# Softmax-off-by-one attention and a maxout feed-forward on one core: the first batch's attention in two query halves, in a hand-made order

## The chip, the cores and the metric

The kernel runs on one NeuronCore of a Trainium2 chip. The metric is the device time of one execution in microseconds (us). Each comparison states the ratio of two kernels: the mean time of one kernel's fast runs over the mean of the other's of the same rounds, with a 95% interval; it is therefore not exactly the ratio of the medians that are quoted beside it. The three batches of experiments were made on different chips, so kernels of two batches are best compared by what each gained on the kernel before in its own batch. The "granted clock" is the share of TensorE's full clock that the throttle let through in an execution. Engines: PE (TensorE, matmuls), ACT (ScalarE), DVE (VectorE), POOL (GpSimd, which here only starts loads), SP (SyncE, starts stores and DMA transposes).

## The reference

Batch 8, 12 heads, 448 tokens, head size 64; then a feed-forward over all 8 x 448 = 3584 tokens of width 768. All inputs and the output are fp32.

```python
scores = scale * np.matmul(q, k.transpose(0, 1, 3, 2))
m = np.max(scores, axis=-1, keepdims=True)
e = np.exp(scores - m)
attn = e / (np.sum(e, axis=-1, keepdims=True) + np.exp(-m) + 1e-09)   # = exp(s) / (1 + sum exp(s))
x = (attn @ v).transpose(0, 2, 1, 3).reshape(B * S, H * D)
h = np.maximum(np.maximum(x @ w1, x @ w2), x @ w3)
out = h @ w_out
```

## The kernel before

The 12 heads of a batch are three groups of four, so there are 24 groups. For each group the kernel makes four "score visits"; each visit issues two key chunks' scores for a pair of heads (PE) and two exponentials (ACT). The denominator and numerator ("AV") of group i-1 are issued in the second visit of group i. Feed-forward "pieces" of the previous batch (18 up-projection pieces, then 6 or 8 output pieces) are put between the visits by a credit of matmul columns, so that PE has work while ACT makes exponentials. A piece of batch b can only be issued when the attention of batch b is complete. So in batch 0 there are no pieces at all.

```python
    ps1 = ctx.enter_context(tc.tile_pool(name="ps1", bufs=4, space=bass.MemoryType.PSUM))  # transposes, AV, pieces
    ps2 = ctx.enter_context(tc.tile_pool(name="ps2", bufs=2, space=bass.MemoryType.PSUM))  # scores, 2 banks each
    ...
    def pair_qk(i):                 # copies of q and k into the order that the transposes want, on DVE
        ...
        for pr in range(GH // 2):
            qk16 = p16_pool.tile([SC, 2, NCH, 2, D], MMDT, tag="qk16", name="qk16")
            for n, t in enumerate((kf, qf)):
                nc.vector.tensor_copy(out=qk16[:, n], in_=t[:, 2 * pr : 2 * pr + 2].rearrange("p h c d -> p c h d"))
    ...
    def av_group(i):
        ...
        den = col_tiled(lambda hh, c: ones16[:, :])
        nc.scalar.activation(out=lnd, in_=den[:, 0:S], func=AF.Ln, bias=one_b)
        nc.scalar.activation(out=rb, in_=lnd, func=AF.Exp, bias=ln_lam, scale=-1.0)
        for hf in range(2):
            num = col_tiled(lambda hh, c: v16[:, hh, c, hf::2])
            nc.vector.tensor_tensor(out=xT[b][:, 2 * g + hf, :], in0=num[:, 0:S], in1=rb, op=ALU.mult)
    ...
    for i in range(NI):
        ...
        gap = (per_group + av_cols + 2 * tr) / 4
        for vi, (pr, cs) in enumerate(visits):
            if vi == 1 and i > 0:
                av_group(i - 1)
            scores_visit(i, pr, cs)
            if vi == 0:
                if on_pe:
                    pair_qk(i + 1)          # all four copies of the next group, ahead of xT's products on DVE
                ...
                moe(gap - av_cols)
            elif vi < 3:
                if vi == 1 and i > 0 and g == 0:
                    add_pieces(b - 1)
                moe((gap - tr) / 2)
                if on_pe:
                    pe_transpose_pair(i + 1, vi - 1)
                moe((gap - tr) / 2)
            else:
                moe(gap)
```

The softmax here doesn't subtract the row's maximum and nothing guards it: scores larger than these inputs give would overflow.

## Time and profile before

The kernel takes 367.57 us (median of 3 runs, 367.45 to 367.81). The profile is of one execution in the slow state (more than 1.5% above the fastest, at a lower granted clock): 407.0 us at a granted TensorE clock of 0.852. Its table of windows gives, for each stretch of the span, the busy time of each engine (with the number of instructions), then the granted clock, the DMA share and GB/s:

```profile
10.00:20.00 10.00, 8.13 (x60) 3.17 (x63) 3.07 (x10) 8.27 (x11) 4.24 (x7) 1.00 1.28 190
30.00:40.00 10.00, 8.02 (x90) 3.37 (x85) 2.50 (x4) 8.02 (x11) 4.16 (x7) 0.74 1.22 205
40.00:50.00 10.00, 10.00 (x70) 4.36 (x62) 5.53 (x12) 3.45 (x4) 4.54 (x7) 0.79 1.28 203
100.00:150.00 50.00, 50.00 (x366) 21.17 (x368) 23.01 (x50) 26.25 (x33) 6.25 (x9) 0.85 0.66 101
350.00:390.00 40.00, 40.00 (x265) 18.46 (x263) 17.50 (x30) 9.51 (x12) 0.00 (x0) 0.85 0.10 31
```

From about 42 us on, PE (first of the busy times) is without a break; ACT (fourth) is about half busy, and less near the end. Before that PE and ACT both show 8 of 10 us. The chain of waits names what sits in that head (start, length, what):

```profile
13.74 3.46 ACT eT L176 x4
17.80 4.13 PE av L196 x47
22.27 4.96 ACT eT L176 x6
27.64 4.08 PE av L196 x48
32.05 4.96 ACT eT L176 x6
37.43 3.91 PE av L196 x48
42.00 2.73 PE p_i L226 x12
56.60 2.74 PE av L196 x48
```

The exponentials (ACT) and the AV blocks (PE) take turns. An AV block takes about 4 us here and 2.74 us later, because PE is at half clock: 93 ns for one of its matmuls is 112 columns (a quarter of 448, as four 32-column tiles run together) at 1.2 GHz. The Trainium skill ("TensorE: Matmul & The Clock Gate", Part 1) says that PE drops to this clock when it has had too little work. The clock column shows 1.00 in the first of these windows although PE is at half clock there: the clock record of this trace begins only with the first change to the higher clock, at 21.1 us.

### The profile page before, as it was taken

How to read it: one execution, taken by the hardware profiler on the slowest of the kernel's cores; microseconds unless marked ns; L12 is line 12 of the kernel's file. 1: busy time of each engine (PE TensorE's matmuls, PEld its weight loads, DVE VectorE, ACT ScalarE, POOL GpSimd, SP SyncE). 2: the span in 40 equal slices, each digit the busy share in tenths (PEclk: the TensorE clock that was granted, in tenths of full speed). 3: DMA queues.
4: the chain of work that ended last, by engine and by line, in shares of the span. 5: the costliest groups of instructions: out<-in, count | busy, mean ns of one | idle time of the engine just before them, and what ended most of it. 6: DMA issues, size and time to landing. Idle time of an engine off the chain costs nothing.

```text
span 407.0 us, 6789 instructions
## 1 busy us (share of the span) xinstructions
PE 389.1 (96%) x2832; PEld 167.4 (41%) x2832; DVE 176.1 (43%) x359; ACT 196.4 (48%) x241; POOL 59.4 (15%) x92
## 2 busy tenths in 40 slices
PE   2888999999999999999999999999999999999995
PEld 1333444443434434344344444444344444344442
DVE  2332554444444444444443444444444443434442
ACT  2887353663644645554545454644645635541000
POOL 8444420220201202201202202202000000000000
PEclk9977888888888888888888888888888888888888
DMA  7999996756838935566437848278212510012005
GB/s 90 192 206 205 202 173 102 110 146 89 112 40 155 156 82 69 89 163 93 75 61 135 150 86 105 54 148 143 48 22 52 156 41 0 2 56 62 0 2 155
DMA packets 73470, 40.94 MB, mean 101 GB/s; under 512 B 35680, under 2 KB 68704, under 8 KB 73440
## 3 DMA queue, kind: packets, MB, share of 16 engines
q0 software_dynamic: 35552, 21.24, 38.0%
q1 hardware_dynamic: 37888, 19.28, 20.7%
q8 instruction: 22, 0.36, 0.4%
q14 instruction: 8, 0.07, 0.1%
HBM read 42.47 MB, written 11.01 MB: 131 GB/s over the span
## 4 chain that ended last, share of the span: by engine, by line
PE 92%; ACT 3%; DMA 2%; POOL 1%; issue 0%; DVE 0%; POOLq 0%
PE p_i L226 48%; PE av L196 17%; PE op_ps L247 16%; PE stp L167 11%; ACT eT L176 3%; DMA ld_k<-in_k_dram 2%; PE trT L141 1%; POOL ld_q L88 1%; POOL ld_k L88 0%; DVE o_sb L254 0%; DVE qk_170 L129 0%; POOL ident_97 masks.py:199 0%; POOL ident_97 masks.py:197 0%; POOLq L366 0%
## 5 line engine op out<-in xcount | busy, mean ns | idle before, releaser
L176 ACT ACTIVATE eT<-stp 112x896 f16<-112x896 f32 x192 | 164.7, 916 | 156.0 <-PE stp L167 156.0
L236 DVE TENSOR_TENSOR hT<-hT,p_i 128x448 f16<-128x448 f16 x96 | 59.6, 621 | 80.6 <-PE p_i L226 80.6
L226 PE MATMUL p_i<-xT,w_122 128*128 128x448 f16 x288 | 70.8, 387 | 0.0
L226 PE MATMUL p_i<-xT,w_123 128*128 128x448 f16 x288 | 70.7, 388 | 0.0
L226 PE MATMUL p_i<-xT,w_124 128*128 128x448 f16 x288 | 70.2, 387 | 0.0
L247 PE MATMUL op_ps<-w_125,hT 128*128 128x384 f16 x336 | 66.5, 358 | 0.0
L167 PE MATMUL stp<-qkT 64*128 64x448 f16 x384 | 59.9, 385 | 5.5 <-ACT eT L176 5.4
L196 PE MATMUL av<-eT,ld_v 112*32 112x448 f16 x768 | 49.5, 408 | 0.0
L254 DVE TENSOR_SCALAR o_sb<-op_ps 128x384 f32<-128x384 f32 x56 | 31.2, 558 | 39.8 <-PE op_ps L247 39.8
L88 POOL DMA_DIRECT2D ld_v<-in_v_dram x24 | 16.8, 702 | 213.1 <-PE stp L167 136.2
L212 DVE TENSOR_TENSOR xT<-av,rb 128x448 f16<-128x448 f32 x48 | 27.9, 620 | 45.1 <-ACT rb L209 37.4
L234 DVE CAST hT<-p_i 128x448 f16<-128x448 f32 x48 | 30.0, 625 | 39.7 <-PE p_i L226 39.7
L247 PEld LDWEIGHTS <-hT 128*128 128x128 f16 x336 | 33.7, 104 | 32.4 <-issue 7.1
L226 PEld LDWEIGHTS <-w_123 128*128 128x128 f16 x288 | 28.6, 104 | 35.3 <-issue 7.3
L226 PEld LDWEIGHTS <-w_124 128*128 128x128 f16 x288 | 27.7, 103 | 36.4 <-issue 9.3
L226 PEld LDWEIGHTS <-w_122 128*128 128x128 f16 x288 | 27.9, 103 | 35.5 <-issue 7.9
L196 PEld LDWEIGHTS <-ld_v 112*32 112x32 f16 x768 | 22.5, 108 | 22.7 <-issue 4.3
L167 PEld LDWEIGHTS <-qkT 64*128 64x128 f16 x384 | 12.1, 95 | 46.7 <-issue 46.1
L196 PE MATMUL av<-eT,ones_116 112*32 112x448 f16 x384 | 25.6, 393 | 0.0
L207 ACT ACTIVATE lnd<-av,one_b 128x448 f32<-128x448 f32 x24 | 15.3, 638 | 14.9 <-PE av L196 14.8
L88 POOL DMA_DIRECT2D ld_q<-in_q_dram x25 | 17.7, 708 | 6.8 <-DMA w_124<-in_moe_w_dram 1.5
L88 POOL DMA_DIRECT2D ld_k<-in_k_dram x25 | 17.5, 698 | 5.2 <-DMA ld_v<-in_v_dram 1.9
(137 smaller groups left out, 84.7 us busy)
## 6 DMA issues: line engine op xcount, KB each, us to landing
ld_v<-in_v_dram POOLq DMA_DIRECT2D x24, 224.0 KB, 4.5
ld_q<-in_q_dram POOLq DMA_DIRECT2D x23, 224.0 KB, 5.6
ld_k<-in_k_dram POOLq DMA_DIRECT2D x23, 224.0 KB, 6.2
out_dram<-o_sb SPq DMA_DIRECT2D x8, 336.0 KB, 2.8
out_dram<-o_sb SPq DMA_DIRECT2D x8, 288.0 KB, 2.6
out_dram<-o_sb SPq DMA_DIRECT2D x8, 240.0 KB, 2.7
out_dram<-o_sb SPq DMA_DIRECT2D x8, 192.0 KB, 2.6
w_122<-in_moe_w_dram POOLq DMA_DIRECT2D x3, 384.0 KB, 10.6
```

What stands on the lines that cost most here:

```text
L88: nc.gpsimd.dma_start(out=tiles[name][:, h0 : h0 + step].rearrange("p h c d -> p h (c d)"), in_=src[:, h0 : h0 + step],)
L141: nc.tensor.transpose(out=trT[:, n, ts(c, SC)], in_=qk16[:, n, c, :, :], identity=ident16[0:SC, 0:SC],)
L167: nc.tensor.matmul(out=stp[:, hh, 0:S], lhsT=qkT[hh * D : hh * D + D, c * SC : c * SC + 128], rhs=qkT[hh * D : hh * D + D, S : 2 * S], sta ...
L176: nc.scalar.activation(out=st["eT"][:, 2 * pr : 2 * pr + 2, c, :], in_=stp[0:SC, :, 0:S], func=AF.Exp, scale=scale,)
L196: nc.tensor.matmul(out=bank[32 * hh : 32 * hh + 32, 0:S], lhsT=weights(hh, c), rhs=eT[:, hh, c, :], start=(c == 0), stop=(c == NCH - 1),)
L207: nc.scalar.activation(out=lnd, in_=den[:, 0:S], func=AF.Ln, bias=one_b)
L212: nc.vector.tensor_tensor(out=xT[b][:, 2 * g + hf, :], in0=num[:, 0:S], in1=rb, op=ALU.mult)
L226: nc.tensor.matmul(out=p_i[:, 0:S], lhsT=w_sb[i][:, dc, ts(fc, 128)], rhs=xT[b][:, dc, :], start=(dc == 0), stop=(dc == NDC - 1),)
L234: nc.vector.tensor_copy(out=dst, in_=p_i[:, 0:S])
L236: nc.vector.tensor_tensor(out=dst, in0=dst, in1=p_i[:, 0:S], op=ALU.max)
L247: nc.tensor.matmul(out=op_ps[:, 0:NW], lhsT=hT[bp][:, fc, ts(t, 128)], rhs=wout_sb[:, fc, ts(nh, NW)], start=(fc == 0), stop=(fc == NFC - 1),)
L254: nc.vector.tensor_scalar(out=o_sb[:, ts(nh, NW)], in0=op_ps[:, 0:NW], scalar1=1.0 / LAMBDA, scalar2=None, op0=ALU.mult,)
```

## The change

The intent is to have feed-forward work for PE earlier. Batch 0's attention is computed for the first 224 queries of all three groups first. Then up-projection pieces for those 224 tokens are legal, and the hand-made order puts seven of them under the second half's exponentials. Besides: the first two heads' q and k come as fp32 over the hardware queues of SP and ACT; group 2's q and k load before group 1's v; the copies for a PE transpose stand right before it; one more group is transposed on PE; and the pieces that are left of batch 0 are spread over groups 3 to 5. The diff has three more parts: more buffers in two pools, another order of the later loads, and, in all later groups, the DMA transposes moved from the first score visit to the third and fourth. The core of the diff (cut):

```diff
-    load_group(0, "qk", 2)
+    for name, src, eng in (("k", k, nc.sync), ("q", q, nc.scalar)):
+        first[name] = cpool.tile([SC, 2, NCH, D], FP32, name="first_" + name)
+        eng.dma_start(out=first[name]..., in_=src[0]...[:, 0:2])
+    load_group(0, "qk", 2, 2)
...
+    load_group(2, "qk")
     load_group(1, "v")
-    load_group(2)
+    load_group(2, "v")
...
+    def scores_half(i, pr, half):      # as scores_visit, 224 queries: 4 pairs of matmuls, 2 exponentials
+    def av_half(i, half):              # as av_group, 224 queries
+    def up_half(b, fp, i, half):       # two fc blocks x 224 tokens in one bank
...
-    PE_TR = 6
+    PE_TR = 7
+    start = """
+        C00 T00 S000 C01 T01 S010
+        C10 T10 C11 S100 T11 A00 S110
+        C20 T20 C21 S200 T21 A10 S210
+        S001 A20 S011 M1 M1 S101 M1 A01 S111 M1
+        C30 C31 S201 A11 T30 M1 S211 T31 M1 A21 M1
+    """                                # C copies, T transposes, S scores, A AV block, M one piece; last digit: half
...
+        if g == 0:
+            per_group = sum(w for f, a, w in pieces) / NG if i == NG else steady
...
             if vi == 0:
-                if on_pe:
-                    pair_qk(i + 1)
                 moe(gap - av_cols)
+            elif vi == 1:
+                moe(gap)
+            else:
+                if tr:
+                    pair_qk(i + 1, vi - 2)
+                moe((gap - tr) / 2)
+                if tr:
+                    pe_transpose_pair(i + 1, vi - 2)
```

More of the change, by code (lines that the diff above doesn't have):

```diff
@@ L60 @@
     p16_pool = ctx.enter_context(tc.tile_pool(name="p16", bufs=4))
-    att_pool = ctx.enter_context(tc.tile_pool(name="att", bufs=6))
-    e_pool = ctx.enter_context(tc.tile_pool(name="e", bufs=2))
+    att_pool = ctx.enter_context(tc.tile_pool(name="att", bufs=8))
+    e_pool = ctx.enter_context(tc.tile_pool(name="e", bufs=3))
     small = ctx.enter_context(tc.tile_pool(name="small", bufs=2))
@@ L74, with load_group @@
     raw = {}
-    def load_group(i, which="qkv", step=GH):
+    def load_group(i, which="qkv", step=GH, start=0):
         b, g = groups[i]
@@ L82, in load_group @@
             )
-        for h0 in range(0, GH, step):
+        for h0 in range(start, GH, step):
             for name in which:
@@ L91, in load_group @@
                 )
-    load_group(0, "qk", 2)
+    HQ = S // 2
+    first = {}
+    for name, src, eng in (("k", k, nc.sync), ("q", q, nc.scalar)):
+        first[name] = cpool.tile([SC, 2, NCH, D], FP32, name="first_" + name)
+        eng.dma_start(
+            out=first[name].rearrange("p h c d -> p h (c d)"),
+            in_=src[0].rearrange("h (p c) d -> p h (c d)", c=NCH)[:, 0:2],
+        )
+    load_group(0, "qk", 2, 2)
     ident16 = cpool.tile([128, 128], MMDT, name="ident16")
@@ L121, with pair_qk @@
     state = {}
-    def pair_qk(i):
-        qf, kf = raw[i].pop("q"), raw[i].pop("k")
-        state[i] = {"qk16": [], "qkT": []}
-        for pr in range(GH // 2):
-            qk16 = p16_pool.tile([SC, 2, NCH, 2, D], MMDT, tag="qk16", name="qk16")
-            for n, t in enumerate((kf, qf)):
-                nc.vector.tensor_copy(
-                    out=qk16[:, n],
-                    in_=t[:, 2 * pr : 2 * pr + 2].rearrange("p h c d -> p c h d"),
-                )
-            state[i]["qk16"].append(qk16)
+    def pair_qk(i, pr):
+        st = state.setdefault(i, {"qk16": {}, "qkT": {}})
+        qk16 = p16_pool.tile([SC, 2, NCH, 2, D], MMDT, tag="qk16", name="qk16")
+        for n, name in enumerate("kq"):
+            if i == 0 and pr == 0:
+                src = first[name]
+            else:
+                src = raw[i][name][:, 2 * pr : 2 * pr + 2]
+            nc.vector.tensor_copy(
+                out=qk16[:, n], in_=src.rearrange("p h c d -> p c h d")
+            )
+        st["qk16"][pr] = qk16
     def pe_transpose_pair(i, pr):
+        if pr not in state.get(i, {"qk16": {}})["qk16"]:
+            pair_qk(i, pr)
         st = state[i]
-        qk16 = st["qk16"][pr]
+        qk16 = st["qk16"].pop(pr)
         trT = ps1.tile([128, 2, S], MMDT, tag="bank1", name="trT")
@@ L146, in pe_transpose_pair @@
         nc.vector.tensor_copy(out=qkT, in_=trT.rearrange("p n s -> p (n s)"))
-        st["qkT"].append(qkT)
+        st["qkT"][pr] = qkT
     def dma_transpose_pair(i, pr):
+        pair_qk(i, pr)
         st = state[i]
@@ L153, in dma_transpose_pair @@
             out=qkT.rearrange("p (n s) -> p n s", s=SC),
-            in_=st["qk16"][pr].rearrange("p n c h d -> p (n c h d)"),
+            in_=st["qk16"].pop(pr).rearrange("p n c h d -> p (n c h d)"),
         )
-        st["qkT"].append(qkT)
+        st["qkT"][pr] = qkT
     def scores_visit(i, pr, cs):
@@ L214, in av_group @@
             )
+    def scores_half(i, pr, half):
+        st = state[i]
+        key = ("eT", half)
+        if key not in st:
+            st[key] = e_pool.tile([SC, GH, NCH, HQ], MMDT, tag="eT", name="eTh")
+        qkT = st["qkT"][pr]
+        q0 = S + half * HQ
+        stps = []
+        for c2 in range(0, NCH, 2):
+            stp = ps2.tile([128, 2, 512], FP32, tag="bank2", name="stp")
+            for j in range(2):
+                c = c2 + j
+                for hh in range(2):
+                    nc.tensor.matmul(
+                        out=stp[:, hh, ts(j, HQ)],
+                        lhsT=qkT[hh * D : hh * D + D, c * SC : c * SC + 128],
+                        rhs=qkT[hh * D : hh * D + D, q0 : q0 + HQ],
+                        start=True,
+                        stop=True,
+                    )
+            stps.append(stp)
+        for n, stp in enumerate(stps):
+            nc.scalar.activation(
+                out=st[key][:, 2 * pr : 2 * pr + 2, 2 * n : 2 * n + 2, :],
+                in_=stp[0:SC, :, 0:S].rearrange("p h (c q) -> p h c q", c=2),
+                func=AF.Exp,
+                scale=scale,
+            )
@@ new lines, in av_half, with col_tiled @@
+    def av_half(i, half):
+        b, g = groups[i]
+        st = state[i]
+        eT, v16 = st[("eT", half)], raw[i]["v"]
+        if g == 0 and half == 0:
+            xT[b] = xt_pool.tile([128, NDC, S], MMDT, tag="xT", name="xT")
+        def col_tiled(out, weights):
+            for c in range(NCH):
+                for hh in range(GH):
+                    nc.tensor.matmul(
+                        out=out[32 * hh : 32 * hh + 32],
+                        lhsT=weights(hh, c),
+                        rhs=eT[:, hh, c, :],
+                        start=(c == 0),
+                        stop=(c == NCH - 1),
+                    )
+        den = ps1.tile([128, 512], FP32, tag="bank1", name="den")
+        col_tiled(den[:, 0:HQ], lambda hh, c: ones16[:, :])
+        lnd = small.tile([128, S], FP32, tag="lnd", name="lnd")
+        nc.scalar.activation(
+            out=lnd[:, 0:HQ], in_=den[:, 0:HQ], func=AF.Ln, bias=one_b
+        )
+        rb = small.tile([128, S], FP32, tag="rb", name="rb")
+        nc.scalar.activation(
+            out=rb[:, 0:HQ], in_=lnd[:, 0:HQ], func=AF.Exp, bias=ln_lam, scale=-1.0
+        )
+        num = ps1.tile([128, 512], FP32, tag="bank1", name="num")
+        for hf in range(2):
+            col_tiled(num[:, ts(hf, HQ)], lambda hh, c: v16[:, hh, c, hf::2])
+        for hf in range(2):
+            nc.vector.tensor_tensor(
+                out=xT[b][:, 2 * g + hf, ts(half, HQ)],
+                in0=num[:, ts(hf, HQ)],
+                in1=rb[:, 0:HQ],
+                op=ALU.mult,
+            )
@@ L236, in up_piece @@
             nc.vector.tensor_tensor(out=dst, in0=dst, in1=p_i[:, 0:S], op=ALU.max)
+    def up_half(b, fp, i, half):
+        if fp == 0 and i == 0 and half == 0:
+            hT[b // 2] = ht_pool.tile([128, NFC, 2 * S], MMDT, tag="hT", name="hT")
+        dst = hT[b // 2][:, 2 * fp : 2 * fp + 2, ts(half, HQ)]
+        p_i = ps1.tile([128, 512], FP32, tag="bank1", name="p_i")
+        for j in range(2):
+            for dc in range(NDC):
+                nc.tensor.matmul(
+                    out=p_i[:, ts(j, HQ)],
+                    lhsT=w_sb[i][:, dc, ts(2 * fp + j, 128)],
+                    rhs=xT[b][:, dc, ts(half, HQ)],
+                    start=(dc == 0),
+                    stop=(dc == NDC - 1),
+                )
+        src = p_i[:, 0:S].rearrange("p (j q) -> p j q", j=2)
+        if i == 0:
+            nc.vector.tensor_copy(out=dst, in_=src)
+        else:
+            nc.vector.tensor_tensor(out=dst, in0=dst, in1=src, op=ALU.max)
     NH = 2
@@ L273, with add_out @@
     pieces = []
-    def add_pieces(b):
-        order = [(fc, i) for fc in range(NFC) for i in range(3)]
-        if b == 0:
-            order = [(fc, i) for i in range(3) for fc in range(NFC)]
-        for fc, i in order:
-            pieces.append((up_piece, (b, fc, i), NDC * (S + 6)))
+    def add_out(b):
         for t in range(0, 3) if b % 2 == 0 else range(3, 7):
@@ L283, in add_pieces @@
                 pieces.append((out_piece, (b // 2, t, nh), NFC * (NW + 6)))
+    def add_pieces(b):
+        for fc in range(NFC):
+            for i in range(3):
+                pieces.append((up_piece, (b, fc, i), NDC * (S + 6)))
+        add_out(b)
     credit = [0.0]
@@ L298 @@
     OUT = NFC * (NW + 6)
-    per_group = (3 * NFC * UP + 3.5 * NH * OUT) / NG
+    steady = (3 * NFC * UP + 3.5 * NH * OUT) / NG
     av_cols = 3 * NCH * (S + 6) + 480
@@ L303 @@
     NI = len(groups)
-    PE_TR = 6
-    pair_qk(0)
-    pe_transpose_pair(0, 0)
-    pe_transpose_pair(0, 1)
-    for i in range(NI):
-        b, g = groups[i]
-        if i == 0:
-            load_weight(0)
-            load_group(3, "qk")
-        elif i == 1:
-            load_weight(1)
-            load_group(3, "v")
-        elif i == 2:
-            load_weight(2)
-            load_group(4)
+    PE_TR = 7
+    UP_H = 2 * NDC * (HQ + 6)
+    load_weight(0)
+    load_weight(1)
+    load_group(3, "qk")
@@ new lines, with add_halves @@
+    load_weight(2)
+    load_group(4, "qk")
+    load_group(3, "v")
+    def add_halves(b, i, half):
+        for fp in range(NFC // 2):
+            pieces.append((up_half, (b, fp, i, half), 1.0))
+    for i, half in ((0, 0), (1, 0), (2, 0), (0, 1), (1, 1), (2, 1)):
+        add_halves(0, i, half)
+    ops = {
+        "C": pair_qk,
+        "T": pe_transpose_pair,
+        "S": scores_half,
+        "A": av_half,
+        "M": moe,
+    }
+    start = """
[4 more added lines that the diff above has]
+        C30 C31 S201 A11 T30 M1 S211 T31 M1 A21 M1
@@ L321 @@
+    """
+    for op in start.split():
+        ops[op[0]](*(int(n) for n in op[1:]))
+    credit[0] = 0.0
+    for i in range(NG):
+        state.pop(i)
+    pieces[:] = [(f, a, UP_H) for f, a, w in pieces]
+    add_out(0)
+    for i in range(NG, NI):
+        b, g = groups[i]
+        if i == 3:
+            load_group(5, "qk")
+            load_group(4, "v")
             load_weight(3)
-            load_group(5)
+            load_group(5, "v")
+            load_group(6)
         elif i + 3 < NI:
@@ L324 @@
             load_group(i + 3)
-        on_pe = i + 1 < PE_TR
-        tr = tr_cols if on_pe else 0
+        tr = tr_cols if i + 1 < PE_TR else 0
+        if g == 0:
+            per_group = sum(w for f, a, w in pieces) / NG if i == NG else steady
         gap = (per_group + av_cols + 2 * tr) / 4
         for vi, (pr, cs) in enumerate(visits):
-            if vi == 1 and i > 0:
+            if vi == 1 and i > NG:
                 av_group(i - 1)
+                if g == 0:
+                    add_pieces(b - 1)
@@ L331 @@
             scores_visit(i, pr, cs)
             if vi == 0:
-                if on_pe:
-                    pair_qk(i + 1)
-                if i + 2 >= PE_TR and i + 2 < NI:
-                    pair_qk(i + 2)
-                    for p2 in range(2):
-                        dma_transpose_pair(i + 2, p2)
-                moe(gap - av_cols)
-            elif vi < 3:
-                if vi == 1 and i > 0 and g == 0:
-                    add_pieces(b - 1)
-                moe((gap - tr) / 2)
-                if on_pe:
-                    pe_transpose_pair(i + 1, vi - 1)
-                moe((gap - tr) / 2)
-            else:
-                moe(gap)
+                moe(gap - av_cols)
+            elif vi == 1:
+                moe(gap)
+            else:
+                if tr:
[3 more added lines that the diff above has]
+                    pe_transpose_pair(i + 1, vi - 2)
+                if i + 2 >= PE_TR and i + 2 < NI:
+                    dma_transpose_pair(i + 2, vi - 2)
+                moe((gap - tr) / 2)
```

## The prediction

> **What bounds the kernel now.** The profiled run spans 407.0 us at a granted clock of 0.852 (slow state); the timed runs take 367.57 us. By the timeline and the windows, PE is busy without a break from about 42 to 402 us. That stretch is bound by matmul columns: 18 up-projection matmuls take 4.04 us, 224 ns each. Stretching only this part by the clock (407.0 to about 365.8 us of span) means roughly 0.96 in the timed runs. The tail after the last exponential (369 to 402 us) is also dense and unchanged.
>
> The head is not dense. Up to 42 us only batch 0's attention is done. It alternates: ACT waits for scores (the wait table up to 80 us: ACT eT behind PE stp 32.0 us, longest 7.3) while PE does a group's whole denominator and numerator (chain: 4.13, 4.08, 3.91 us, against 2.71 later). These blocks are slow because PE is at its half clock: 93 ns per matmul is 112 columns at 1.2 GHz. The Trainium skill ("TensorE: Matmul & The Clock Gate", Part 1) says that PE falls to 1.2 GHz after idle windows; this trace agrees by that 93 against 56 ns. Its useful PE work is about 16 us, so some 24 us are lost.
>
> **What the change does.** Same FLOPs. Half of batch 0's queries need 12 exponentials of about 0.83 us pitch (916 ns each) instead of 24 before feed-forward pieces become legal; the other 12 run under 7 half-width pieces. PE's blocks get half as long, so ACT starves less. The first two heads come by hardware queues in fp32; group 2's q,k move ahead of group 1's v.
>
> **Costs.** 24 ns per half-width AV matmul is ideal, but weight loads show about 33 ns spacing in the trace (16 in 0.53 us): I estimate 0.45 us extra for each of six blocks, 2.7 us. One more group is transposed on PE (2 x 0.59 us). Narrow pieces: 0.3 us. DVE reads fp32 for the first copy: below 0.5 us.
>
> **Loads.** About 205 KB/us of fp16 land. By that estimate w1's first matrix lands near 23 us, the second near 29, the third near 37; they are needed near 29, 33 and 42. No wait expected. Group 1's q,k (near 10 us) remain an early wait.
>
> **Estimate.** Placing the new order by hand with the trace's durations, the first half piece starts near 28 us and the hand-made order ends near 45 us with 7 pieces done. Seven pieces are 8.4 us at the clock 0.96, so it equals a dense start at 36.6 us against 41.3 before: 4.7 us gained. Less the extra transposes and narrow pieces: 3.3 us; plus about 1 us for faster first loads: about 4.5 us. The rate change only moves work: PE has no idle time there to win.
>
> Predicted 363.0 us; range 359.0 to 366.5. Faster by over 2%: 0.2; within 2%: 0.79; slower: 0.01.
>
> **What would show it.** First half piece at 26 to 31 us; ACT's wait for scores before 45 us about halved; PE unbroken from there; half AV blocks at 1.3 to 1.7 us once warm; no PE wait for weight DMAs; the rest as before.
>
> **What would make it wrong.** PE staying at half clock until 25 us or later (loses 1 to 2 us); half-width AV at ideal speed, or PE warm from 17 us (gains 1 to 3 us); weights late; a granted clock that answers to the denser head; stalls of PE in groups 3 to 5, where fewer pieces are spread over the same exponentials.

## The result, and the profile after

The changed kernel takes 363.13 us (median of 4 runs, 362.5 to 363.52); the ratio to the kernel before is 0.9877 (95% interval 0.986 to 0.9894). All its runs were at a granted clock of 0.997 to 0.999. In a later batch it gave 363.21 us and 0.9888 (0.9868 to 0.9909).

The windows of the changed kernel:

```profile
10.00:20.00 10.00, 7.95 (x150) 5.96 (x152) 4.54 (x13) 7.44 (x11) 3.95 (x7) 1.00 1.26 204
20.00:30.00 10.00, 8.21 (x152) 6.26 (x148) 3.06 (x7) 8.29 (x13) 3.83 (x6) 1.00 1.17 209
30.00:40.00 10.00, 9.93 (x213) 8.11 (x202) 5.42 (x15) 7.85 (x12) 4.64 (x8) 1.00 1.29 200
40.00:50.00 10.00, 8.74 (x87) 6.63 (x86) 4.93 (x12) 5.70 (x7) 4.81 (x8) 1.00 1.29 204
100.00:150.00 50.00, 50.00 (x428) 22.43 (x427) 24.98 (x51) 30.27 (x38) 7.41 (x11) 1.00 0.66 111
```

Its timeline around the first pieces (start, length, engine, line, operation, operands, count, idle time before it and what ended that):

```profile
18.95 0.57 PE L269 MATMUL den<-eTh,ones_118 112*32 112x224 f16 x16
19.35 0.94 PE L269 MATMUL num<-eTh,ld_v 112*32 112x224 f16 x32
20.22 0.56 PE L243 MATMUL stp<-qkT 64*128 64x224 f16 x8
24.66 0.56 PE L327 MATMUL p_i<-xT,w_124 128*128 128x224 f16 x4
25.50 2.28 PE L327 MATMUL p_i<-xT,w_124 128*128 128x224 f16 x20 [0.28 <-DVE xT L291]
40.78 0.55 PE L180 MATMUL stp<-qkT 64*128 64x448 f16 x4
42.15 0.37 PE L180 MATMUL stp<-qkT 64*128 64x448 f16 x2 [0.82 <-ACT eT L189]
```

The first half piece starts at 24.66 us, the hand-made order is done at 40.78 us. A half AV block takes 1.27 us (18.95 to 20.22), about half of a full one (2.39 us in b_again, below).

The two profiles are of different states. So the first experiment was the kernel before once more, for a profile at full clock (b_again, span 365.4 us). All comparisons of traces below use it.

### Where the time came from

PE's busy time does not tell a matmul at half clock from one at full clock. I therefore counted, from each trace, the matmul work that had been started by a given time. One matmul counts its columns at 2.4 GHz plus 2.4 ns, divided by two for the 64-row tiles of the scores and by four for the 32-column tiles of AV. (Check: in b_again the 448-column up-projection matmuls start 189.0 ns apart in the median, and 448 / 2.4 + 2.4 = 189.1; in the changed kernel's trace the 224-column ones start 96 ns apart and the 112-column transposes 49 ns, where the formula gives 95.7 and 49.1.) The table is this calculation, in us of work done by the matmuls that had started; the last column is the start of the last matmul plus its own work:

| by time | 10 | 20 | 30 | 42 | 50 | 80 | 340 | all work | last matmul ends |
|---|---|---|---|---|---|---|---|---|---|
| before (b_again) | 1.2 | 4.8 | 9.7 | 16.2 | 23.6 | 51.6 | 293.3 | 313.4 | 360.3 |
| changed kernel | 1.6 | 6.5 | 13.3 | 23.0 | 29.7 | 56.7 | 299.2 | 314.6 | 355.6 |
| lead | 0.4 | 1.7 | 3.6 | 6.8 | 6.1 | 5.1 | 5.9 | -1.2 | 4.7 |

The whole gain is made before 42 us: a lead of 6.8 us. It is partly given back: 1.7 us between 42 and 80 us (groups 3 to 5), and 1.2 us because there is more work (one more group of transposes, and the fixed part of each of the narrower matmuls). ACT does the same amount by 40 us in both: added over the four windows, 26.95 us busy in b_again and 26.87 in the changed kernel. So ACT was not made faster. What changed is that PE did seven pieces beside it: 84 matmuls, 8.0 us by this count.

### The profile page after: what moved, and what is told of

It is laid out like the page before. It is cut to its first block, busy times and chain, and to the rows that moved or that the text cites. A ratio compares the mean times of both kernels' runs of the same rounds, so it can differ in the third digit from the quotient of the medians.

```text
span 360.7 us, 7434 instructions
## 1 busy us (share of the span) xinstructions
PE 343.3 (95%) x3148; PEld 173.5 (48%) x3148; DVE 177.5 (49%) x367; ACT 197.3 (55%) x247; POOL 58.1 (16%) x90
## 4 chain that ended last, share of the span: by engine, by line
PE 89%; ACT 5%; DVE 3%; DMA 1%; issue 1%; DVEq 0%
PE p_i L308 40%; PE op_ps L349 16%; PE av L209 11%; PE stp L180 11%; PE p_i L327 6%; PE trT L153 2%; ACT eTh L252 2%; ACT eT L189 1%; PE stp L243 1%; DVE xT L225 1%; DMA first_k<-in_k_dram 1%; PE num L269 1%; ACT rb L222 1%; ACT lnd L220 1%; DVE qkT L158 1%
## 5 line engine op out<-in xcount | busy, mean ns | idle before, releaser
L189 ACT ACTIVATE eT<-stp 112x896 f16<-112x896 f32 x168 | 144.7, 914 | 106.6 <-PE stp L180 106.6
L318 DVE TENSOR_TENSOR hT<-hT,p_i 128x448 f16<-128x448 f16 x84 | 52.2, 621 | 56.6 <-PE p_i L308 55.5
L349 PE MATMUL op_ps<-w_127,hT 128*128 128x384 f16 x336 | 59.0, 327 | 0.0
L308 PE MATMUL p_i<-xT,w_124 128*128 128x448 f16 x252 | 55.3, 353 | 0.4
L308 PE MATMUL p_i<-xT,w_126 128*128 128x448 f16 x252 | 54.8, 354 | 0.0
L308 PE MATMUL p_i<-xT,w_125 128*128 128x448 f16 x252 | 54.7, 353 | 0.0
L180 PE MATMUL stp<-qkT 64*128 64x448 f16 x336 | 46.6, 355 | 1.3 <-ACT eT L189 1.3
L308 PEld LDWEIGHTS <-w_125 128*128 128x128 f16 x252 | 23.4, 98 | 27.0 <-issue 7.0
L308 PEld LDWEIGHTS <-w_126 128*128 128x128 f16 x252 | 22.9, 98 | 27.0 <-issue 7.8
L308 PEld LDWEIGHTS <-w_124 128*128 128x128 f16 x252 | 23.3, 98 | 25.9 <-issue 5.9
L209 PE MATMUL av<-eT,ld_v 112*32 112x448 f16 x672 | 35.4, 353 | 0.0
L252 ACT ACTIVATE eTh<-stp 112x896 f16<-112x896 f32 x24 | 20.5, 912 | 10.8 <-PE stp L243 10.7
L209 PEld LDWEIGHTS <-ld_v 112*32 112x32 f16 x672 | 18.0, 97 | 13.8
L209 PE MATMUL av<-eT,ones_118 112*32 112x448 f16 x336 | 19.7, 355 | 0.0
L220 ACT ACTIVATE lnd<-av,one_b 128x448 f32<-128x448 f32 x21 | 13.3, 635 | 9.4 <-PE av L209 9.4
```

What stands on the lines that cost most here:

```text
L180: nc.tensor.matmul(out=stp[:, hh, 0:S], lhsT=qkT[hh * D : hh * D + D, c * SC : c * SC + 128], rhs=qkT[hh * D : hh * D + D, S : 2 * S], sta ...
L189: nc.scalar.activation(out=st["eT"][:, 2 * pr : 2 * pr + 2, c, :], in_=stp[0:SC, :, 0:S], func=AF.Exp, scale=scale,)
L209: nc.tensor.matmul(out=bank[32 * hh : 32 * hh + 32, 0:S], lhsT=weights(hh, c), rhs=eT[:, hh, c, :], start=(c == 0), stop=(c == NCH - 1),)
L252: nc.scalar.activation(out=st[key][:, 2 * pr : 2 * pr + 2, 2 * n : 2 * n + 2, :], in_=stp[0:SC, :, 0:S].rearrange("p h (c q) -> p h c q", ...
L308: nc.tensor.matmul(out=p_i[:, 0:S], lhsT=w_sb[i][:, dc, ts(fc, 128)], rhs=xT[b][:, dc, :], start=(dc == 0), stop=(dc == NDC - 1),)
L318: nc.vector.tensor_tensor(out=dst, in0=dst, in1=p_i[:, 0:S], op=ALU.max)
```

## The experiments

Theory: the gain comes from PE having legal feed-forward work under the second half's exponentials. Rivals: the gain comes from the loads; from PE being kept at full clock; from the copies on DVE.

### b_again: the kernel before at full clock

No edit.

> The kernel before, unchanged, for a trace in the fast state. If the recorded 0.85 clock only stretched the dense part, its head ends again near 42 us and the dense part takes about 306 us, which would leave some 12 us of the 367.57 unaccounted; so I expect either a head longer than 42 us or gaps of PE after it. Half-clock blocks of denominator and numerator (about 4 us each) are expected again in the head.

Measured: 367.17 us, span 365.4, granted clock 0.995 (a single run, so its state is called unknown; the fast runs of the kernel before in that batch have a median of 367.65 us). The head is not longer than in the slow profile: the dense part starts at 42.26 us. So the dense part takes 318 us (42.3 to 360.3) at full clock, where I had reckoned 306. Two things make up most of the difference (both are measured below): between the two traces a 448-column matmul shrinks by 1.153 and not by 1.174, and the stops at changes of PE's tiling mode (the scores use tiles of 64 rows of PE's array, AV tiles of 32 columns, the pieces the whole array) keep their length. The dense part has 179 such changes of about 95 ns, 17 us; the other 343 of its 360 us, shrunk by 1.153, give 297 us, so 314 us together. Some 4 us stay unexplained. The profile also shows a wait that I had read over in the slow trace. DVE, then PE:

```profile
36.85 0.94 PE L196 MATMUL av<-eT,ones 112*32 112x448 f16 x16
39.24 0.55 PE L167 MATMUL stp<-qkT 64*128 64x448 f16 x4
40.24 0.29 DVE L129 COPY qk<-ld_k 112x512 f16<-112x512 f16 x1 [5.38 <-DMA ld_k<-in_k_dram]
41.05 1.15 DVE L212 TENSOR_TENSOR xT<-av,rb 128x448 f16<-128x448 f32 x2
41.73 0.35 PE L226 MATMUL p_i<-xT,w 128*128 128x448 f16 x1 [1.07 <-DVE xT L212]
```

The product that completes batch 0's xT stands on DVE behind the copies for group 4, which wait for group 4's k. AV is done at 39.24 us and its reciprocal (ACT, rb) at 39.35 us, but the product starts only at 41.05 us. The Trainium skill ("Perfetto Trace Analysis", section "Tensor Engine Instruction (MATMUL, LD_WEIGHTS)") says that DVE is strictly first in, first out; this trace agrees.

Its windows show the half clock as a granted clock below 1 (third value from the end, 0.87 and 0.96):

```profile
20.00:30.00 10.00, 7.91 (x92) 3.53 (x88) 3.56 (x8) 8.46 (x11) 4.06 (x7) 0.87 1.17 207
30.00:40.00 10.00, 7.91 (x105) 3.44 (x95) 2.50 (x4) 8.11 (x11) 4.16 (x7) 0.96 1.23 205
40.00:50.00 10.00, 8.75 (x60) 4.19 (x59) 6.15 (x13) 4.23 (x6) 4.56 (x8) 1.00 1.28 203
```

The clock records in the trace put full clock at 20.6 to 27.4 us, half clock at 27.4 to 30.8 us, then full clock until PE's work is over. The changed kernel is at full clock from 15.2 us until its work is over.

### w_warm: keep PE warm in the old order

```diff
+        if i in (1, 2) or (i == 0 and pr == 1):          # in scores_visit
+            warm = ps1.tile([128, 512], FP32, tag="bank1", name="warm")
+            for _ in range(3):
+                nc.tensor.matmul(out=warm[:, 0:S], lhsT=qkT[:, 0:128], rhs=qkT[:, S : 2 * S], start=True, stop=True)
```

> The kernel before plus three matmuls without use after each scores visit of groups 1 and 2 and of the second pair of group 0, where PE waits for ACT anyway. Theory 1 (the change gains because feed-forward starts after half of the exponentials): no gain, 0 to 1 us slower. Rival (the change gains mostly because PE is kept at full clock in the head): faster by 2 to 4 us, with numerator blocks near 2.4 us instead of about 4 us.

Measured: 368.6 us, ratio 1.0034 (0.9999 to 1.0069): no gain. This does not rule the rival out, because another wait swallowed it. PE is warm from 15.2 us and the AV blocks take 2.4 us, so PE is ready earlier, but it then stands longer behind DVE's queue and cools down:

```profile
38.51 0.55 PE L167 MATMUL stp<-qkT 64*128 64x448 f16 x4
38.99 0.93 PE L233 MATMUL p_i<-xT,w 128*128 128x448 f16 x4
42.67 3.30 PE L233 MATMUL p_i<-xT,w 128*128 128x448 f16 x8 [2.74 <-DVE xT L219]
```

The clock record of this trace shows half clock at 42.5 to 46.0 us. So the test had to be repeated with that wait removed (g_copies, g_warm).

### f_loads and u_loads: the loads alone, and undone

f_loads is the kernel before with the two load hunks of the diff above; u_loads is the changed kernel with `load_group(0, "qk", 2)` in place of the fp32 loads; group 2's q and k still load before group 1's v in it.

> The kernel before with only the new first loads (first two heads in fp32 by the hardware queues, group 2's q and k before group 1's v). If the loads are a main part of the gain: 2 to 4 us faster than before. By my theory about 1 us, since the first exponentials start only about 0.5 to 2 us earlier and the head is then paced by ACT and by the blocks of PE.

> The changed kernel with the old first loads (first pair of heads by the software queue again). By my theory it keeps 3 us or more of the 4.4 us gain; if the loads are a main part, only 0 to 2 us are left.

Measured: f_loads 366.92 us, ratio 0.998 (0.9957 to 1.0003), which is not clear of no effect. u_loads 365.23 us, ratio 0.9954 (0.9914 to 0.9994), with runs from 364.07 to 369.3. The loads are worth 0.7 us at most in the old order, but taking the fp32 loads out of the new one costs about 2 us (the intervals of u_loads and of the changed kernel do not meet); the expectation of "3 us or more" kept was a miss (2.4 us kept by the medians). In u_loads' trace, against the changed kernel's, the second pair's copies start at 7.20 us and not at 6.47, group 1's at 11.61 and not 9.59, and the first half piece at 26.83 and not 24.66. PE also becomes warm later there, at 18.9 us and not at 15.2. So the first loads matter more in the new head than in the old one; how much of this is their landing and how much is PE's clock was not separated.

### g_copies and g_warm: the copies moved, and warmth again

g_copies is the kernel before with the copies moved; g_warm has the three useless matmuls of w_warm besides.

```diff
             if vi == 0:
-                if on_pe:
-                    pair_qk(i + 1)
...
             elif vi < 3:
+                if on_pe:
+                    pair_qk(i + 1, (vi - 1,))
                 moe((gap - tr) / 2)
```

> The kernel before with one thing moved: each copy of q and k that feeds a transpose on PE stands right before that transpose in program order, not at the group's first visit. In the fast trace of the kernel before, VectorE holds group 2's product for xT behind such copies, which wait 5.38 us for group 4's k; PE then stands 1.07 us in its first up-projection. If this queueing is part of the loss: 1 to 2 us faster than before (about 366), and no stop of PE between the first up pieces. If not: no change.

> The same move of the copies plus the three matmuls without use of the run w_warm, so that a longer wait of VectorE can no longer hide what warmth is worth. Rival (PE at half clock is the main loss of the head): 2 us or more faster than the run g_copies. My theory (ACT's exponentials and their order pace the head): within 1 us of g_copies.

Measured: g_copies 366.45 us, ratio 0.996 (0.993 to 0.999); g_warm 365.57 us, ratio 0.9933 (0.9909 to 0.9957). Both are faster than the kernel before. The windows of g_copies, then those of g_warm:

```profile
20.00:30.00 10.00, 7.97 (x96) 3.39 (x92) 3.37 (x8) 8.53 (x12) 3.67 (x6) 0.86 1.17 207
30.00:40.00 10.00, 7.92 (x92) 3.39 (x88) 3.69 (x9) 7.84 (x11) 4.23 (x6) 0.84 1.23 205
```

```profile
20.00:30.00 10.00, 9.30 (x112) 3.89 (x100) 3.63 (x9) 8.48 (x11) 3.47 (x6) 1.00 1.17 206
30.00:40.00 10.00, 9.36 (x101) 4.23 (x98) 4.18 (x10) 9.39 (x12) 4.22 (x6) 1.00 1.23 205
```

In g_copies the stop before the pieces is gone (its up pieces start at 41.41 us without a wait), but PE falls to half clock twice. In g_warm it stays at full clock from 14.7 us to the end, and the pieces start at 38.60 us. So the copies bring about 1 us and warmth about 0.9 us more by the medians (the two intervals overlap), within the 1 us that my theory allowed; not the 2 us or more that the rival claimed. One rival was not run: the kernel before with the loads, the copies and the warmth together. Added up, 0.7 and 1.9 us would be 2.6 of the 4.4 us, but that these sizes add up in the old order is not shown.

### h_noint: halves without pieces between

```diff
-        S001 A20 S011 M1 M1 S101 M1 A01 S111 M1
-        C30 C31 S201 A11 T30 M1 S211 T31 M1 A21 M1
+        S001 A20 S011 S101 A01 S111
+        C30 C31 S201 A11 T30 S211 T31 A21
+        M1 M1 M1 M1 M1 M1 M1
```

> The changed kernel with the seven feed-forward pieces of the hand-made order moved behind all of batch 0's attention: halves without interleaving. By my theory (the gain is feed-forward under the second half's exponentials) the gain is lost: 367 us or slower, PE standing 5 us or more between 24 and 40 us. If half blocks, loads and copies alone bring the gain: near 363 to 364.

Measured: 366.73 us, ratio 0.9988 (0.9951 to 1.0024). All the other parts of the change are in this kernel, the untested ones too, and by the medians it gains 0.75 us on the kernel before in its batch where the changed kernel gained 4.4: about 3.7 us are gone. The "367 us or slower" was missed by 0.3 us, and PE stood still for 3.2 us between 24 and 40 us (12.80 of 16 us busy), not for 5; the mean granted clock of that stretch is 0.89, so part of what counts as busy is half-clock work. Its trace:

```profile
26.57 0.37 PE L243 MATMUL stp<-qkT 64*128 64x224 f16 x4 [1.15 <-ACT eTh L252]
27.67 0.94 PE L269 MATMUL den<-eTh,ones 112*32 112x224 f16 x16
28.40 1.71 PE L269 MATMUL num<-eTh,ld_v 112*32 112x224 f16 x32
37.72 8.22 PE L327 MATMUL p_i<-xT,w 128*128 128x224 f16 x84
```

The seven pieces (84 matmuls) come in one block of 8.22 us after the exponentials. Without them PE waits for ACT and also falls to half clock (27.7 to 31.1 us in the clock record), so that an AV block takes 2.4 us (27.67 to 30.04, where the next scores start). By the work count h_noint stands at 18.9 us of work at 42 us, in the middle of its block, and at 52.4 us at 80 us; the changed kernel has 23.0 and 56.7. The pieces between the exponentials are the gain; part of what they do is to keep PE warm, and how large that part is was not separated.

### c_credit and r_steady: the rate of pieces

At group 3's first visit the changed kernel subtracts the AV block's columns from the credit, although no AV block follows there. PE stands at 41 to 43 us (the lines of 40.78 and 42.15 above).

```diff
-                moe(gap - av_cols)
+                moe(gap if i == NG else gap - av_cols)        # c_credit
...
-            per_group = sum(w for f, a, w in pieces) / NG if i == NG else steady
+            per_group = steady                                # r_steady
```

> The changed kernel with one mend: at group 3's first visit the credit is not reduced by the AV columns, because no AV block follows there (group 2's was in the hand-made order). In the changed kernel's trace PE issues no piece between the two score visits and stands about 1.3 us at 41 to 43 us. I expect 0.8 to 1.5 us faster than the changed kernel, about 362.

> The changed kernel with the last part undone: groups 3 to 5 use the steady rate of pieces instead of what is left of batch 0. My theory: the rate only moves work, so equal within 0.5 us; the higher rate puts a piece between group 3's first two score visits (gains about 1.3 us at 41 to 43 us), and runs out of pieces in group 5, where PE then waits for ACT (loses 1 to 3 us). If the rate by what is left matters: 2 us or more slower than the changed kernel, with PE waiting in group 5.

Measured: c_credit 362.96 us, ratio 0.9874 (0.9844 to 0.9904): the same as the changed kernel, so the expected 0.8 to 1.5 us were a miss. r_steady 364.08 us, ratio 0.992 (0.9895 to 0.9945), beside 0.9888 (0.9868 to 0.9909) for the changed kernel in the same batch (run a_again): 0.9 us slower by the medians, with overlapping intervals, which is neither the "within 0.5 us" nor the "2 us or more" of its expectation.

> The changed kernel, unchanged, beside the three kernels below on the same chip, as their reference: 363 us, 0.988 of the kernel before.

The mend works where it was made and is paid for later. By the work count c_credit leads a_again by 0.5 us at 50 us (29.8 against 29.3) and by 0.0 us at 80 us (56.6 both). What was won at 41 us is lost at 74 to 75 us, where the pieces of batch 0 have run out. c_credit there, then r_steady, which runs out still earlier:

```profile
73.35 0.56 PE L153 MATMUL trT<-ident,qk 112*128 112x112 f16 x8
73.84 0.58 PE L180 MATMUL stp<-qkT 64*128 64x448 f16 x4
75.30 0.57 PE L153 MATMUL trT<-ident,qk 112*128 112x112 f16 x8 [0.87 <-DVE qk L140]
```

```profile
71.30 0.55 PE L180 MATMUL stp<-qkT 64*128 64x448 f16 x4
72.67 0.36 PE L180 MATMUL stp<-qkT 64*128 64x448 f16 x2 [0.82 <-ACT eT L189]
73.48 0.37 PE L180 MATMUL stp<-qkT 64*128 64x448 f16 x2 [0.44 <-ACT eT L189]
```

There are 11 half pieces and 6 output pieces for three groups. In all three ways of dealing them that were run, PE waits somewhere before batch 1's pieces become legal; the rate decided where.

### x_warm and x_both: PE warmed before the data land

```diff
+    busy16 = cpool.tile([128, S], MMDT, name="busy16")
+    nc.vector.memset(busy16, 1.0)
...
+    def busy(n):                                # "W": n matmuls without use, 448 columns each
...
-        C00 T00 S000 C01 T01 S010
-        C10 T10 C11 S100 T11 A00 S110
-        C20 T20 C21 S200 T21 A10 S210
+        W9 C00 T00 W1 S000 C01 T01 W1 S010
+        W2 C10 T10 W2 C11 S100 T11 A00 S110
+        C20 T20 W2 C21 S200 T21 A10 S210
```

> The changed kernel plus matmuls without use on a constant tile: nine before the first data land, and one or two in the gaps of about 0.7 us around the first transposes. In the changed kernel's traces PE runs at half clock until 15 to 19 us. If warmth of PE paces the first 15 us: full clock from about 8 us on and 1 to 2 us faster than the changed kernel. If the landing of data and ACT pace them: no gain, or 0.5 us slower.

> The run x_warm plus the mended credit at group 3's first visit. Expected 0.5 to 1.5 us faster than x_warm, about 361; if ACT takes the gain back later, equal to x_warm.

Measured: x_warm 361.74 us, ratio to the kernel before 0.985 (0.9822 to 0.9878); x_both 361.86 us, 0.9848 (0.9824 to 0.9872). The changed kernel in the same batch: 363.21 us, 0.9888 (0.9868 to 0.9909). So x_warm is 1.5 us faster than the changed kernel by the medians; the two intervals overlap a little, from 0.9868 to 0.9878. The mended credit brings nothing here either, where 0.5 to 1.5 us had been expected; the expectation named that case too, but put it down to ACT, which no trace was asked to show. The timeline of x_warm:

```profile
1.39 3.54 PE L430 MATMUL junk<-busy 128*128 128x448 f16 x9 [1.39 <-DVE ln_lam L117]
6.45 0.56 PE L245 MATMUL stp<-qkT 64*128 64x224 f16 x8 [0.53 <-DVE qkT L160]
12.80 0.57 PE L271 MATMUL den<-eTh,ones 112*32 112x224 f16 x16
13.20 0.94 PE L271 MATMUL num<-eTh,ld_v 112*32 112x224 f16 x32
24.03 0.56 PE L329 MATMUL p_i<-xT,w 128*128 128x224 f16 x4
```

PE is at full clock from 5.4 us by the clock record, and the first scores take 0.56 us, where they took 0.93 us in the changed kernel's trace. At the first piece 0.6 us is left (24.03 against 24.66 us). The two profiled executions differ by about as much (361.82 against 362.50 us); where the rest of the 1.5 us between the medians comes from was not separated. The profiled run of x_both fell to half clock once more, at 12.4 to 15.8 us, while it waited 1.60 us for group 1's q and k.

## Why the prediction was right or wrong

The forecast of 363.0 us met 363.13 us, and its mechanism was shown: h_noint loses 3.7 of the 4.4 us. But several sizes in its sum were off and balanced each other, so it is luck that it came within 0.2 us: two things of which the prediction had said that either would gain 1 to 3 us more both happened (half AV blocks at nearly ideal speed, PE warm before 17 us), and groups 3 to 5 gave much of it back.

- **Clock (wrong).** I took 0.96 as the clock of the timed runs, because I shrank the whole dense part by the clock. All fast runs have a granted clock of 0.985 to 1.0. The dense part takes 318 us at full clock, not 306: a 448-column matmul goes from 218 to 189 ns, a factor of 1.153 and not 1 / 0.852 = 1.174, and the stops at changes of tiling mode stay the same. The forecast was a difference to 367.57 us, so little of this error reached it (the seven pieces are 8.0 us and not 8.4).
- **Half AV blocks (mis-sized).** I added 0.45 us for each of six blocks, from a spacing of weight loads of 33 ns. Measured is 1.27 us for 48 matmuls, 26.5 ns each, against 2.39 us for a full block: 0.07 us extra. That holds for the five blocks after PE is warm and makes 1.9 us; the first, nearly all of it at half clock, takes 2.16 us (13.35 to 15.51).
- **When PE becomes warm (mis-sized).** The prediction counted on something between 17 and 25 us, as it names both ends as errors; it was 15.2 us in the first trace. Together with the previous point this fits that the first piece came at 24.66 us and not near 28 (outside the 26 to 31 us that I gave), and the hand-made order ended at 40.78 us and not at 45.
- **The head before (step missed).** I read its end, 42 us, rightly, but not what it ends with in b_again: a stop of PE (1.07 us and 0.18 us) behind DVE's queue and group 4's load. g_copies shows that this is worth about 1 us.
- **"PE has no idle time there to win" (wrong).** Groups 3 to 5 lose 1.7 us of the lead. I had named these stalls only as a risk. c_credit and r_steady show that they move with the rate but don't go away.
- **ACT's wait about halved (wrong).** Before 45 us, the wait table of b_again has 11.3 us of ACT behind scores, and that of the changed kernel 10.7 + 1.3. ACT is as busy by 40 us as before.
- **Loads (right in size for the old order).** About 1 us expected, 0.7 measured alone (with an interval that includes no effect); within the new order they are worth about 2 us. No wait of PE for a weight's DMA appears after the change, as expected.
- **Extra work (right).** 1.4 us expected for transposes and narrow pieces, 1.2 us counted.

So a lead of 6.8 us where I had 4.7 plus 1, and 2.9 us given back where I had 1.4, less 0.8 us that the later part wins by the count: the sum is 4.7 us in the traces.

## What to carry to other kernels

Where one engine's long stage must finish before another's work becomes legal, cutting the first stage so that half of its result is complete early lets the other engine work under the second half; here that was about 3.7 us. Measure it as work done by a given time, not as busy time. A finite stock of filler work may not close every gap: here dealing it out differently only moved the wait. Before a large reordering, look for copies that wait for loads at the head of an in-order queue, and for stretches in which PE is too idle to keep its clock: each was worth about 1 us here by the medians for a few lines, the second not clear of noise by itself.

## What the Trainium skill lacked or had wrong

- "TensorE: Matmul & The Clock Gate", Part 1, says in its table that PE falls back to half clock after an idle window; further down it tells of a kernel whose short idle times were enough. It gives no share of work at which this happens. Here PE fell back while it was working: in b_again it went to half clock at 27.4 us after a stretch (20.6 to 27.4 us) with matmul work of 48% by my count and no stop over 0.44 us. No limit comes out of that count: the changed kernel stayed warm through 15.2 to 22.0 us with 50% and c_credit through 16.7 to 23.5 us with 46%, while g_copies fell at 37.5 us after a stretch of 6.8 us with 50%.
- The same part tells that the window is free-running, so that the moment of the change varies from run to run. No run here isolates this, but the traces fit it: the changed kernel was warm from 15.2 us in one trace and 15.6 us in another, and c_credit, whose program is the same up to 40 us, from 16.7 us. No page gives the spread of a whole kernel: r_steady's executions with a granted clock of 0.998 or 0.999 took 363.44 to 364.1 us, those with 0.987 took 365.85 and 366.19 us.
- The same part has 13/16 as the limiter's clock and needs three busy cores. This program has one core, and its slow run has 0.850 in the clock record for all of the dense part. Whether this is the page's limiter is not known, nor what the other cores of the chip did.
- Part 2 ("Back-to-back issue gap") gives about 131 ns for each 512-column matmul in a stream of weight loads and matmuls. Here 448 columns take 189.0 ns in the median, which is 448 / 2.4 + 2.4: the formula that the page gives for isolated matmuls holds in the stream.
- Part 4 says that the full clock does not engage for transposes in PE's transpose mode. Here, once other matmuls have warmed PE, they get it: eight 112-column transposes (`nc.tensor.transpose`, listed as MATMUL) take 0.93 us when PE is cold and 0.57 us when it is warm, and start 93 and 49 ns apart. Whether transposes alone would warm PE is not shown.
- "TensorEngine Tiling (Array Packing)", Key Properties, says that changing the tiling mode drains the array, without a size. Between 110 and 290 us of b_again, in the median, the first score matmul starts 285 ns after an up-projection matmul, and the next up-projection matmul 282 ns after the last scores, against 189 ns between two up-projections: about 95 ns each way (280 to 285 ns in all 61 such places). Where the mode stays the same there is no such stop: an output matmul starts 189 ns after an up-projection. That the drain is the cause is inferred from this. In the slow trace these are 315 and 311 ns against 218: nearly the same 95 ns, so this part does not shrink with the clock.
